# Even spacing of early attention scores among the dense matmuls

## The chip, the cores and the metric

The kernel runs on one core of a Trainium2 chip. A core has a matrix engine (PE, with its weight loads listed as PEld), a vector engine (DVE), a scalar engine (ACT), a general engine (POOL), and a queue that mostly issues DMAs (SP). They run their own instruction streams and wait for each other by semaphores. Matmul results land in PSUM, which is cut into eight banks of 128 x 512 fp32; only DVE and ACT can read them out. The metric is the device time of one execution in microseconds; less is better.

## The reference, cut to what matters

One attention block and one dense block with a gate, over the same normalised input of 2048 tokens by 512:

```python
xn  = layernorm(x)                                  # 2048 x 512
q, k, v = split(xn @ wqkv, heads=32)                # 16 wide each
p   = softmax(q @ k.T * 16 ** -0.5)                 # 32 heads, 2048 x 2048
s   = (p @ v).reshape(2048, 512) @ wo
h   = gelu(xn @ w1 + b1)                            # 2048 x 1376
g   = silu(h @ w2 + b2)
out = x + s * g
```

All of it is fp32. The kernel holds that precision by splitting an operand into a high and a low part and adding three products (high x high, high x low, low x high).

## The kernel before, in words

The softmax needs the maximum of each row of scores before the exponentials. The kernel therefore makes every block of scores twice: once with the queries on the PSUM partitions, only to take row maxima (the *score matmuls*, `s_mm`, line 184, read by a DVE max over 128 x 512, `s_max`, line 190), and once with the keys on the partitions, with the maxima folded in, for the exponentials on ACT (`t_one`, lines 716 and 718).

There are two large stages. In the *dense stage* PE does the value projection, the remaining query and key projections and both dense layers. In the *attention stage* it makes scores, exponentials and the products with the values. The row maxima of the first nine of 32 units (a unit is four heads by 512 queries) are made early, spread through the dense stage: `LEAD = 144` counts the blocks, and each block takes four score matmuls, two heads of a pair and two pairs, so 4 x 144 = 576 *early score tiles*.

A dense matmul contracts over 64 rows, half of the array, and its two halves run as two streams, *row tile* 0 (operand partitions 0 to 63) and row tile 1 (64 to 127). The function `run` (line 595) takes two lists of dense matmuls, one for each row tile, and issues them by turns: one for tile 0, one for tile 1, and so on. Ahead of each it calls `fill(a)` (line 564) with the tile `a` whose turn it is; `fill` may put in one early score on that row tile, which contracts over 48 rows. It does so when the count of what has been issued reaches a due value, and when it is that tile's turn among the scores (`made[0] <= made[1]` picks tile 0, otherwise tile 1), so that even scores are on tile 0 and odd ones on tile 1. `mm` (line 584) issues the dense matmul (line 590) and counts it; where a dense sum was last written by the other row tile and no early score since proves that write done, it first puts in an empty PE instruction that waits for it.

A score tile is written to one of two PSUM banks by turns (`s_ring`, line 91). Each score thus needs the bank that the score two before it used, and its weight load waits on PE until DVE has taken that one's max. The ring is the only link between the scores and DVE.

When the maxima of two units are complete, `s_end0` (line 239) reduces them and queues a transpose that `fill` puts in place of a score some scores later (`later`, `s_end1`, line 268); it takes the next bank of the ring, ACT reads it out (`s_end2`, line 276), and SP stores it to a scratch in DRAM (`mh_d`, line 279), which the attention stage loads (line 152). Four of these fall into the dense stage. `put` raises the due value for each of them.

The due value before is made from `ROWS`, the count of row-half slots in the whole stage, 12 steps for each half of each projection pair, 6 for each part of the second layer, and the scores themselves. Each tile has its own count `row[a]`, which dense matmuls and scores of that tile both raise. The order of everything in the dense stage is thus fixed when the program is built; nothing is decided on the chip.

The other engines in the dense stage: ACT and POOL split weights and hidden activations into high and low parts and read out the sums of the first layer (lines 297, 298, 371, 373, 377, 378), SP loads weights and stores queries and keys. At the end of the stage DVE adds a bias to the last four sums (line 649).

Of the kernel before, what the change touches and what calls it, by code (L numbers as in the profile page):

```python
# [32 lines left out]
LEAD = 144  # L33
NW = 10
EARLY = 4
DONE = 492
FILL0 = 30
HB = 4
W2B = 2
ORDER = {0: "TTTTV", 3: "TSXTTSTYV"}  # L40
# [9 lines left out]
def fused(ctx: ExitStack, tc: tile.TileContext, x, wqk, wv, wo, w1, b1, w2, b2, out):  # L50
# [104 lines left out]
    made = [0, 0]  # L155
# [6 lines left out]
    def tick():  # L162
        for e in later:
            e[0] -= 1
# [39 lines left out]
    def s_one(a):  # L204
        made[a] += 1
        s_whole(heads[made[a] - 1], a)
# [58 lines left out]
    def s_end1(u):  # L265
        pm = s_tile()[0] if "seen" in prog or u == NU - 1 else t_tile()
        n = 2 * GH * NCH * len(units_of(u))
        nc.tensor.matmul(pm[:n, :P], NM.pop(u).rearrange("p u i a -> p (u i a)"), ident_r, start=True, stop=True)
        MH[u] = pm

    def s_end2(u):
        us = units_of(u)
        n = 2 * GH * NCH * len(us)
        mh = qring.tile([4 * GH * NCH, P], F32, name="mh", bufs=1)
        if "seen" in prog:
            nc.scalar.activation(mh[:n], MH.pop(u)[:n, :P], AF.Copy)
        else:
            nc.vector.tensor_copy(mh[:n], MH.pop(u)[:n, :P])
        nc.sync.dma_start(mh_d[us[0]:us[-1] + 1].rearrange("u i j (q s) -> (u i j q) s", s=P), mh[:n])
        sent.update(us)  # L280
# [21 lines left out]
    VQ = 3  # L302
    first = [[("v", t // NCH, t % NCH) for t in range(i, i + 4)] for i in range(NT - 4 * VQ, NT, 4)]
    qs = [(2, 0), (2, 2)] + [(g, 0) for g in range(3, NG)] + [(g, 2) for g in range(3, NG)]
    nu, pairs = len(ms) // 2, []
# [7 lines left out]
    plan, nd = [("first", g, i) for g in range(VQ - 1) for i in (0, 2)], 0  # L313
    for j in range(len(pairs)):
        for h in range(2):
# [4 lines left out]
            due = next((i for i in range(j, len(pairs)) if is_m[i]), len(pairs))  # L320
# [46 lines left out]
    def evac(us, ph):  # L367
# [6 lines left out]
        for u, raw in zip(us, raws):  # L374
            hh = wk.tile([P, CH], F32R, name="hh", bufs=HB)
            hl = wk.tile([P, CH], F32R, name="hl", bufs=HB)
            nc.scalar.activation(hh, raw, AF.Copy)  # L377
# [179 lines left out]

    prog.update(n=0, pe=0, seen=0)
    writer = {}
    s_when, put, row = [], [0], [0, 0]  # L560
    ndown = sum(1 for e in plan if e[0] == "down")
    ROWS = 12 * (4 * VQ + 2 * len(pairs)) + 6 * ndown - 10 + 2 * LEAD - 2 * (LEAD // 32) - FILL0

    def fill(a):
        due = FILL0 + put[0] + sum(made) * ROWS // (4 * LEAD)
        if sum(made) < 4 * LEAD and row[a] >= due and (made[0] <= made[1]) == (a == 0):
            taken()
            if later and later[0][0] <= 0:
                put[0] += 2
                u = later.pop(0)[1]  # L570
                s_end1(u)
                s_end2(u)
                return
            s_one(a)
            row[a] += 1
            tick()

    def taken():
        prog["pe"] += 1
        s_when.append(prog["pe"])  # L580
        if len(s_when) > 2:
            prog["seen"] = max(prog["seen"], s_when[-3])

    def mm(a, key, ps, lhs, rhs, first, last):
        r = slice(64 * a, 64 * a + 64)
        if not first and writer[key][0] != a and writer[key][1] > prog["seen"]:
            hold = nc.tensor.nop().ins
            tc.add_manual_dep(hold, writer[key][2], SYNC, reason="other row tile")
            prog["seen"] = writer[key][1]
        i = nc.tensor.matmul(ps, lhs[r], rhs[r], start=first, stop=last).ins  # L590
        prog["pe"] += 1
        row[a] += 1
        writer[key] = (a, prog["pe"], i.name)

    def run(ops, hooks={}):
        for n, two in enumerate(zip(*ops)):
            prog["n"] += 1
            for a in range(2):
                fill(a)
                mm(a, *two[a])  # L600
            for h in hooks.get(n, []):
                h()
# [448 lines left out]
```

## Time and profile before

| | us |
|---|---|
| median of 3 runs (1572.62 to 1572.99) | 1572.92 |
| the profiled execution | 1573.31 |
| its span, first to last instruction | 1571.4 |
| first to last early score (start) | 58.62 to 471.53 |
| PE, DVE, ACT, POOL busy in the span | 1564.2, 1397.1, 1233.8, 371.9 |
| the 2048 maxes on DVE (line 190) | 1298.8 |

How to read the rows: a timeline row has the start and the length in us, the engine, the line of the kernel, the operation, output and inputs by the program's names, the tile's shapes, and how many instructions were merged (x4). In brackets stands the idle time of that engine just before, and who ended it. Rows of groups have the busy time and the mean in ns of one, then the idle time before them. Ends of matmuls are modelled, so starts are safer to read than ends. Line numbers are those of the kernel before.

### The profile page before, as it was taken

How to read it: one execution, taken by the hardware profiler on the slowest of the kernel's cores; microseconds unless marked ns; L12 is line 12 of the kernel's file. 1: busy time of each engine (PE TensorE's matmuls, PEld its weight loads, DVE VectorE, ACT ScalarE, POOL GpSimd, SP SyncE). 2: the span in 40 equal slices, each digit the busy share in tenths (PEclk: the TensorE clock that was granted, in tenths of full speed). 3: DMA queues.
4: the chain of work that ended last, by engine and by line, in shares of the span. 5: the costliest groups of instructions: out<-in, count | busy, mean ns of one | idle time of the engine just before them, and what ended most of it. 6: DMA issues, size and time to landing. Idle time of an engine off the chain costs nothing.

```text
span 1571.4 us, 31849 instructions
## 1 busy us (share of the span) xinstructions
PE 1564.2 (100%) x12264; PEld 952.0 (61%) x12264; DVE 1397.1 (89%) x2290; ACT 1233.8 (79%) x2397; POOL 371.9 (24%) x394
## 2 busy tenths in 40 slices
PE   9999999999999999999999999999999999999998
PEld 7899999999994444444444444444444444444455
DVE  7599898989988999999999999999999999999834
ACT  4333333333339999999999999999999999999984
POOL 4145575766741001001100100100010000000143
PEclk9999999999999999999999999999999999999999
DMA  6626343454322114111511511321061111110163
GB/s 208 152 59 150 122 139 99 141 152 120 131 84 75 42 30 71 32 36 38 82 32 32 69 33 40 51 52 29 21 81 29 33 29 31 42 30 22 45 199 111
DMA packets 74648, 116.87 MB, mean 74 GB/s; under 512 B 23013, under 2 KB 24293, under 8 KB 73321
## 3 DMA queue, kind: packets, MB, share of 16 engines
q1 hardware_dynamic: 70748, 101.89, 24.1%
q0 software_dynamic: 3264, 12.35, 4.7%
q8 instruction: 97, 1.59, 0.4%
q10 hardware_dynamic: 484, 0.60, 0.1%
q14 instruction: 55, 0.44, 0.1%
HBM read 84.35 MB, written 25.97 MB: 70 GB/s over the span
## 4 chain that ended last, share of the span: by engine, by line
PE 98%; DVE 1%; ACT 0%; DMA 0%; issue 0%; DVEq 0%
PE pv L781 33%; PE pst L716 20%; PE ps L590 13%; PE ps L184 12%; PE pst L590 7%; PE ps L716 6%; PE pv L590 2%; PE ps L905 1%; PE ps L81 1%; PE ps L459 1%; PE pst L81 1%; DVE st L418 0%; PE pst L441 0%; DMA xt<-in_x 0%; PE pst L459 0%
## 5 line engine op out<-in xcount | busy, mean ns | idle before, releaser
L190 DVE TENSOR_REDUCE mx<-ps 128x2 f32<-128x512 f32 x2048 | 1298.8, 685 | 113.7 <-PE ps L184 45.5
L718 ACT ACTIVATE slot<-pst 128x512 f32<-128x512 f32 x1533 | 826.0, 603 | 14.0 <-PE pst L716 7.5
L781 PE MATMUL pv<-slot,vsb 128*32 128x512 f32 x4096 | 545.3, 605 | 0.3 <-DVE os L788 0.3
L716 PE MATMUL pst<-qt,kt 50*128 50x512 f32 x1149 | 380.3, 430 | 0.6 <-DVE gt L649 0.4
L184 PE MATMUL ps<-kt,slot 48*128 48x512 f32 (+1 forms) x1364 | 377.4, 367 | 0.0
L716 PEld LDWEIGHTS pst<-qt,kt 50*128 50x128 f32 x1149 | 191.6, 184 | 256.8 <-ACT slot L718 240.4
L718 ACT ACTIVATE slot<-ps 128x512 f32<-128x512 f32 x515 | 310.9, 604 | 1.9 <-PE ps L184 0.5
L184 PEld LDWEIGHTS ps<-kt,slot 48*128 48x128 f32 x1364 | 225.5, 184 | 40.3 <-DVE mx L190 35.2
L590 PE MATMUL ps<-slot,w1h 64*128 64x512 f32 x1088 | 217.8, 393 | 0.0
L184 PE MATMUL ps<-kt,qz 48*128 48x512 f32 x512 | 213.7, 417 | 0.0
L184 PE MATMUL ps<-slot,slot 48*128 48x512 f32 (+1 forms) x598 | 165.7, 366 | 0.0
L716 PE MATMUL ps<-qt,kt 50*128 50x512 f32 x387 | 160.0, 416 | 0.0
L590 PEld LDWEIGHTS ps<-slot,w1h 64*128 64x128 f32 x1088 | 154.4, 185 | 4.6
L590 PE MATMUL ps<-slot,w1l 64*128 64x512 f32 x544 | 142.0, 393 | 0.0
L781 PEld LDWEIGHTS pv<-slot,vsb 128*32 128x32 f32 x4096 | 80.7, 108 | 100.3 <-issue 92.3
L378 POOL TENSOR_TENSOR hl<-hg,hh 128x512 fp32r<-128x512 f32 x76 | 96.8, 1296 | 151.5 <-ACT hh L377 99.7
L371 ACT ACTIVATE hg<-ps,b_sb 128x512 f32<-128x512 f32 x44 | 27.8, 684 | 132.7 <-PE ps L590 116.9
L251 POOL CAST nmh<-nm 128x16 fp32r<-128x16 f32 x32 | 6.3, 196 | 489.1 <-DVE nm L248 466.6
L716 PE MATMUL pst<-qt,slot 50*128 50x512 f32 x384 | 111.3, 415 | 0.0
L184 PEld LDWEIGHTS ps<-slot,slot 48*128 48x128 f32 x598 | 98.8, 184 | 17.2 <-DVE mx L190 15.2
L184 PEld LDWEIGHTS ps<-kt,qz 48*128 48x128 f32 x512 | 93.7, 183 | 18.7
L716 PEld LDWEIGHTS ps<-qt,kt 50*128 50x128 f32 x387 | 71.1, 184 | 37.5 <-ACT slot L718 31.9
(165 smaller groups left out, 1715.7 us busy)
## 6 DMA issues: line engine op xcount, KB each, us to landing
raw<-in_w SPq DMA_DIRECT2D x88, 256.0 KB
qk_h<-hh SPq DMA_DIRECT2D x32, 256.0 KB
qk_l<-hl SPq DMA_DIRECT2D x32, 256.0 KB
qt<-qk_h SPq DMA_DIRECT2D x128, 64.0 KB
slot<-qk_h SPq DMA_DIRECT2D x92, 64.0 KB
g_d<-gt POOLq DMA_DIRECT2D x16, 256.0 KB, 3.5
qt<-qk_l SPq DMA_DIRECT2D x64, 64.0 KB
dn<-den_d SPq DMA_DIRECT2D x32, 128.0 KB
```

Of the source, the lines that this page charges most:

```text
L81: nc.tensor.matmul(ps, lhs[a], rhs[b], start=first and n == 0, stop=last and n == 2)
L184: return nc.tensor.matmul(ps[:, c0:c0 + w], QS[u][r, p, qi * P:(qi + 1) * P], kts[u // NCH % KB][p][r, k0:k0 + w], start=True, stop=True).ins
L190: nc.vector.tensor_reduce(MX[u][:, 2 * p:2 * p + 2, qi, ki][:, heads, parts], ps.rearrange("p (n c) -> p n c", c=HC), axis=AX.X, op=OP.max)
L251: nc.gpsimd.tensor_copy(hl[:, 0], nm)
L371: nc.scalar.activation(raw, ph.pop(u), AF.Gelu_apprx_tanh, bias=b1_sb[:, u[2]:u[2] + 1])
L378: nc.gpsimd.tensor_sub(hl, raw, hh.bitcast(F32))
L459: nc.tensor.matmul(pq["q", g, c], W1[g][i][:, k * P:(k + 1) * P], (xh, xl)[j][c][:, k], start=n == 0 and k == 0, stop=n == 2 and k == KT - 1)
L590: i = nc.tensor.matmul(ps, lhs[r], rhs[r], start=first, stop=last).ins
L716: nc.tensor.matmul(ps, kts[g % KB][p][r, k * P:(k + 1) * P], QT[u][r, p, :], start=True, stop=True)
L718: nc.scalar.activation(PT[u, k][:, 2 * p + a, :], ps, AF.Exp, scale=SCALE)
L781: nc.tensor.matmul(PV[u][32 * j:32 * j + 32, :], vsb[:, k, h:h + 32], PT[u, k][:, j, :], start=(k == 0), stop=(k == NT - 1))
L905: HALF[0] = nc.tensor.matmul(PW[i][0], OTS[i, k][x][r], (wo_h, wo_l)[y][r, k], start=k == 0 and side == 0 and n == 0, stop=k == KT - 1 and ...
```

## The change

The rule by which `fill` puts a score in is replaced. Before, each row tile has a count of what was issued on it, its scores included, and a score is due at 30 plus 3 for each score made (the value of `ROWS // (4 * LEAD)`) plus 2 for each transpose. After, there is one count, of the dense matmuls of both tiles, and a score or a transpose is due at 60 plus `APART = 5` for each of either made. The alternation between row tiles, the scores' order, the ring and everything else are as they were.

```diff
+APART = 5
...
-    s_when, put, row = [], [0], [0, 0]
-    ndown = sum(1 for e in plan if e[0] == "down")
-    ROWS = 12 * (4 * VQ + 2 * len(pairs)) + 6 * ndown - 10 + 2 * LEAD - 2 * (LEAD // 32) - FILL0
-
+    s_when, put, row = [], [0], [0]
     def fill(a):
-        due = FILL0 + put[0] + sum(made) * ROWS // (4 * LEAD)
-        if sum(made) < 4 * LEAD and row[a] >= due and (made[0] <= made[1]) == (a == 0):
+        due = 2 * FILL0 + APART * (put[0] + sum(made))
+        if sum(made) < 4 * LEAD and row[0] >= due and (made[0] <= made[1]) == (a == 0):
             taken()
             if later and later[0][0] <= 0:
-                put[0] += 2
+                put[0] += 1
                 u = later.pop(0)[1]
                 s_end1(u)
                 s_end2(u)
                 return
             s_one(a)
-            row[a] += 1
             tick()
...
         prog["pe"] += 1
-        row[a] += 1
+        row[0] += 1
         writer[key] = (a, prog["pe"], i.name)
```

## The prediction

> **What bounds the kernel now.** I read the page first, then the busy time by stages, then the groups of one stage, then its timeline engine by engine.
>
> ```profile
> span 1571.4 us, 31849 instructions
> ...
> PE 1564.2 (100%) x12264; PEld 952.0 (61%) x12264; DVE 1397.1 (89%) x2290; ACT 1233.8 (79%) x2397; POOL 371.9 (24%) x394
> ...
> PE 98%; DVE 1%; ACT 0%; DMA 0%; issue 0%; DVEq 0%
> ```
>
> PE is on the chain that ended last for 98% of the span, but a busy PE row only says that some matmul was in flight. The change touches the dense stage alone, so the span is cut there.
>
> ```profile
> 58.60:471.50 412.90, 412.90 (x3473) 378.63 (x3471) 371.50 (x583) 143.52 (x263) 234.55 (x206) 1.00 0.42 120
> ...
> 474.80:1571.40 1096.60, 1091.79 (x8444) 522.91 (x8440) 990.77 (x1621) 1061.17 (x2080) 112.40 (x157) 1.00 0.23 50
> ```
>
> The columns are PE, PEld, DVE, ACT and POOL busy, each with its count, then clock, DMA share and GB/s. The first stretch runs from the first early score to the last: 412.9 us at full clock, ACT and POOL far from full, DVE at 371.5 (90%). The second is the attention phase, which the change leaves as it is.
>
> ```profile
> L190 DVE TENSOR_REDUCE mx<-ps 128x2 f32<-128x512 f32 x576 | 371.7, 686 | 56.6 <-PE ps L184 18.4 <-PE ps L590 7.8 <-PE pst L590 3.5
> ```
>
> In the stage each of the 576 scores has a max on DVE, and DVE idles 56.6 us before them (15.5 of it before the first). So neither engine is full: PE waits for DVE, DVE for PE. How shows in 2 us of the stage.
>
> ```profile
> 300.30 0.42 PE L184 MATMUL ps<-kt,qz 48*128 48x512 f32 x1
> 300.41 0.39 PE L590 MATMUL pst<-w2l,hh 64*128 64x512 f32 x1
> 300.56 0.39 PE L590 MATMUL pv<-w2l,hh 64*128 64x512 f32 x1
> ...
> 300.79 0.39 PE L590 MATMUL pv<-w2h,hl 64*128 64x512 f32 x1
> 300.87 0.44 PE L184 MATMUL ps<-kt,qz 48*128 48x512 f32 x1
> 301.02 0.52 PE L590 MATMUL pst<-w2h,hh 64*128 64x512 f32 x2
> 301.26 0.52 PE L590 MATMUL pst<-w2l,hh 64*128 64x512 f32 x2
> 301.49 0.52 PE L590 MATMUL pst<-w2h,hl 64*128 64x512 f32 x2
> 301.72 0.40 PE L184 MATMUL ps<-kt,qz 48*128 48x512 f32 x1
> ...
> 302.32 0.40 PE L184 MATMUL ps<-kt,qz 48*128 48x512 f32 x1
> ```
>
> Two streams run side by side, one on each half of the array's rows (row tile 0 and 1). The score at 300.30 and the one at 301.72 are on tile 1. Its stream starts at 300.30, 300.56, 300.79, 301.02, 301.26, 301.49, 301.72: a step of 0.26 behind the score, then five of 1.16/5 = 0.232. A whole round of two scores and ten dense matmuls took 1.42 us, against 6 x 0.232 = 1.39 without the long step. The whole stage says the same once the four places are taken off where a small transpose takes the place of a score:
>
> ```profile
> 156.68 0.41 PE L184 MATMUL ps<-kt,qz 48*128 48x512 f32 x1
> ...
> 158.32 0.28 PE L268 MATMUL ps<-ident_r,nmh 128*64 128x128 f32 x1
> ...
> 159.10 0.39 PE L184 MATMUL ps<-kt,qz 48*128 48x512 f32 x1
> ```
>
> Here a round took 2.42 us, 1.0 more. So 575 gaps in 412.9 - 4.0 us, or 408.9/287.5 = 1.422 us a round.
>
> ```profile
> 58.39 0.18 PEld L184 LDWEIGHTS ps<-kt,qz 48*128 48x128 f32 x1
> ...
> 300.21 0.18 PEld L184 LDWEIGHTS ps<-kt,qz 48*128 48x128 f32 x1
> 300.32 0.19 PEld L590 LDWEIGHTS pv<-w2l,hh 64*128 64x128 f32 x1
> ...
> 300.81 0.18 PEld L184 LDWEIGHTS ps<-kt,qz 48*128 48x128 f32 x1
> ...
> 301.62 0.18 PEld L184 LDWEIGHTS ps<-kt,qz 48*128 48x128 f32 x1
> ...
> 302.21 0.18 PEld L184 LDWEIGHTS ps<-kt,qz 48*128 48x128 f32 x1
> ...
> 471.47 0.18 PEld L184 LDWEIGHTS ps<-slot,qz 48*128 48x128 f32 x1
> ```
>
> ```profile
> 299.46 1.29 DVE L190 TENSOR_REDUCE mx<-ps 128x2 f32<-128x512 f32 x2
> ...
> 300.87 1.29 DVE L190 TENSOR_REDUCE mx<-ps 128x2 f32<-128x512 f32 x2
> ...
> 302.31 0.69 DVE L190 TENSOR_REDUCE mx<-ps 128x2 f32<-128x512 f32 x1 [0.15 <-PE ps L590]
> ```
>
> The pair of maxes from 300.87 ends at 300.87 + 1.29 = 302.16, and the next weight load of a score starts at 302.21. The pair before ends at 300.75, the load is at 300.81. The first max of the pair ends at 300.87 + 0.69 = 301.56, the load is at 301.62. Scores own two PSUM buffers, so each load waits for the max two scores back and starts 0.05 us after its end: so do 566 of the 576 loads between the first (58.39) and the last (471.47). A late load is paid by the dense matmul behind it: its own load can start only 0.11 after the score's (300.21, 300.32), and its matmul 0.24 later (300.56). So it starts 0.35 after the score's load, or 0.232 after the score's matmul, whichever is later; a score's load must lead its matmul by 0.12 to cost nothing. The four above lead by 0.09, 0.06, 0.10 and 0.11.
>
> **The change part by part.** The order of the program is counted when it is built; I worked both rules through. Before, ROWS is 1728, so a score is due every 3 counts of its own half, its own scores included: the scores stand ahead of dense matmul 60, 67, 70, 77, 80: gaps of 7 and 3. After, 60, 65, 70, 75: always 5. Even scores (tile 0) stay, odd ones (tile 1) move two dense matmuls ahead. All 576 scores, 2976 dense matmuls and four transposes remain; no instruction, DMA or wait is added or removed; the 12 places where PE waits for the other tile's writer stay 12. On SP and POOL nothing moves but the transpose's read-out and its small store, up to four dense matmuls later (each transpose raises the count by 5 instead of 4).
>
> ```profile
> 435.70 0.45 SPq L279 DMA_DIRECT2D mh_d<-mh  x1
> ...
> 457.70 1.41 SPq L152 DMA_DIRECT2D qt<-mh_d  x2
> ```
>
> I cost that at nothing: the last of these stores is issued 22 us before the first read of what they write, and uncovered it would be 4 x 0.12 = 0.5 us once. The last score has 21 dense matmuls behind it instead of 23:
>
> ```profile
> 471.53 0.43 PE L184 MATMUL ps<-slot,qz 48*128 48x512 f32 x1
> ...
> 474.49 0.69 DVE L649 TENSOR_TENSOR gt<-pv,b_sb 128x512 f32<-128x512 f32 x1 [1.66 <-PE pv L590]
> ```
>
> DVE had been idle 1.66 us ahead of its next work there, which covers the 0.23 by which the last max comes later. So the sum is a matter of the round's length.
>
> Call G the time from a score's matmul to the release of its buffer (start of its max, plus the max, plus 0.05). If every score of a tile is held by its buffer, a round lasts T = (G + 0.35 + 5 x 0.232)/2 = (G + 1.51)/2: the load comes G behind the last score's matmul, and the dense chain runs on from the load. Before, for the score at 300.87: its max is the second of the pair, from 300.87 + 1.29 - 0.69 = 301.47, so 0.60 after the matmul; G = 0.60 + 0.69 + 0.05 = 1.34, T = 1.425. That is the 1.422 measured. Its max is late because DVE is still on the max of the score only three dense matmuls ahead: maxes follow one another no faster than 1.29 - 0.69 = 0.60, the two scores stand 0.57 apart (300.30, 300.87), and the first one's max itself starts 0.57 late.
>
> How soon a max starts that does not queue is seen at the head of the stage, where DVE was idle:
>
> ```profile
> 57.25 0.39 PE L590 MATMUL pv<-kt,slot 64*128 64x512 f32 x1
> ...
> 58.39 0.40 PE L590 MATMUL pv<-kt,slot 64*128 64x512 f32 x1
> ...
> 58.62 0.39 PE L184 MATMUL ps<-kt,qz 48*128 48x512 f32 x1
> ...
> 59.32 0.39 PE L184 MATMUL ps<-kt,qz 48*128 48x512 f32 x1
> ...
> 59.55 0.39 PE L590 MATMUL pst<-kt,slot 64*128 64x512 f32 x1
> 59.55 0.39 PE L590 MATMUL pv<-kt,slot 64*128 64x512 f32 x1
> ```
>
> ```profile
> 59.05 0.69 DVE L190 TENSOR_REDUCE mx<-ps 128x2 f32<-128x512 f32 x1 [15.52 <-PE ps L184]
> ...
> 60.02 0.69 DVE L190 TENSOR_REDUCE mx<-ps 128x2 f32<-128x512 f32 x1 [0.27 <-PE pv L590]
> ```
>
> 58.62 to 59.05: 0.43. But 59.32 to 60.02: 0.70, with DVE idle. The second score is on tile 1, and the dense matmul ahead of it in the program is on tile 0, which ran a step behind and started it only at 59.55. The same holds at 300.30: the dense matmul ahead of it started at 300.41, and the max at 300.87, 0.46 after that. So a score counts as done only when the one ahead of it is, and a lag of tile 0 of 0.11 puts its max 0.57 behind its matmul, with DVE idle (0.15 before 302.31).
>
> The Trainium skill, "TensorE: Matmul & The Clock Gate", Part 3 (packing small matmuls), states that matmuls start and also end in program order. The ends agree with these rows, the starts do not (300.30 stands behind 300.41 in the program). By the whole rule no lag between the tiles could arise, every max would start 0.43 after its matmul, and the new order would give the same 1.39 round as below; where only the ends keep order, the lag is the danger, and it is the slower rival.
>
> With gaps of five, scores stand three steps apart, 0.70, above the 0.60 that DVE needs: no max queues behind another. Then G is 0.43 + 0.69 + 0.05 = 1.17 on the tile that leads, and 1.20 plus the lag on the other. A load leads its matmul by enough when G is at most 1.39 - 0.12 = 1.27, so up to a lag of 0.07. A tile that is not held runs at 1.39; one held by a longer lag runs slower, which shortens its lead over the late tile, so the lag shrinks until neither is held. I take 1.395 (0.2325 a step): 0.027 less a round, times 287.5 = 7.8 us. Bounds: no gain if the lag stays where it is; at most the step of the dense matmuls before any score, (58.39 - 57.25)/5 = 0.228, so 1.368 a round and 15.5 us. I take the step of the stage since it comes from the same mix of matmuls.
>
> Against the profiled execution, 1573.31 us, the sum is 1565.5; that execution lies 0.4 above the median of the runs, so 1565.2 is predicted. The attention phase keeps its 1096.6 us.
>
> **The rivals.**
> - The tiles fall into step: 1.368 a round, 1573 - 15.5 = 1557.4. For it: the head of the stage ran so. Against it: steps of 0.232 in all of the stage, in both tiles.
> - Nothing gained: the odd scores' maxes started late with DVE idle, which more room on DVE does not mend. If the lag of 0.11 stays, G = 0.57 + 0.69 + 0.05 = 1.31, T = 1.41, a gain of 3.4 us at most; with 0.13 it is 1.42, so between 1569.5 and 1573.
> - Slower: the tiles settle a full step apart, as at 59.32. Then every odd max starts 0.70 after its matmul, G = 1.44, T = 1.475, 0.053 a round more, 15.2 us: 1588. It decides from a max that starts 0.59 behind its matmul. For it: it was seen once, and the odd score stays right behind a tile 0 matmul. Against it: the tile that is held slows down, which closes the lag.
>
> **How the numbers follow.** No change can be told from one of 0.2%, 3.1 us. Chances: the forecast 0.57 (its own range 1562 to 1568, steps of 0.231 to 0.234), in step 0.10, nothing gained 0.15, slower 0.18. Faster is the first two, 0.67, and a hair of the third: 0.68; same 0.14; slower 0.18. The range 1557 to 1573.5 leaves out the slower rival alone.
>
> **What would show it.** In the profile after: score matmuls 0.70 apart throughout; score loads that no longer start 0.05 after a max's end but earlier by their place in the stream; the step behind a score 0.23 like the others; no more pairs of maxes in 1.29 us but each with a short idle; the last dense matmul near 467 instead of 474.7. The prediction is wrong if the loads are still released by the maxes, above all if maxes start 0.6 us or more behind their matmuls.

## The result, and the profile after

| | before | after |
|---|---|---|
| median of six runs, us | 1572.97 | 1567.09 |
| lowest and highest | 1572.62 to 1573.60 | 1566.67 to 1567.32 |
| profiled execution, its span | 1573.31, 1571.4 | 1567.11, 1565.3 |
| first to last early score | 58.62 to 471.53 | 59.14 to 466.08 |
| last dense matmul starts | 474.81 | 469.07 |

The ratio is 0.9962, with a 95% interval of 0.9949 to 0.9975: 5.9 us less, where 7.8 were forecast. The busy time by stages of the kernel after, with the columns of before (PE, PEld, DVE, ACT, POOL busy, clock, DMA share, GB/s):

```profile
59.14:466.10 406.96, 406.96 (x3477) 373.55 (x3474) 392.61 (x583) 144.22 (x264) 234.71 (x206) 1.00 0.42 122
...
469.30:1565.30 1096.00, 1091.29 (x8441) 522.57 (x8439) 990.42 (x1621) 1060.72 (x2079) 112.62 (x157) 1.00 0.22 50
```

The stretch of the early scores went from 412.9 to 407.0 us. The attention phase kept its length, 1096.0 against 1096.6. So all of the gain lies where the change is. DVE's busy time in the stretch rose from 371.5 to 392.6 us, although it has the same 576 maxes to take. The group of the maxes says why (in the lines of the changed kernel the max is L191, the score L185, the dense matmul L587):

```profile
L191 DVE TENSOR_REDUCE mx<-ps 128x2 f32<-128x512 f32 x576 | 392.9, 692 | 29.5 <-PE ps L185 19.1 <-PE ps L587 1.3
```

Before, every second max (283 of them) started 0.084 us before the one ahead had ended, and overlapped time counts once: 576 maxes of 686 ns make 395 us, but only 371.7 us of busy time. Now 253 maxes overlap their neighbour, by 0.022 us in the median, and the idle time is 29.5 us instead of 56.6, 15.5 of it before the first. A busier DVE here is the same work spread out. The timeline of PE after:

```profile
298.66 0.40 PE L185 MATMUL ps<-kt,qz 48*128 48x512 f32 x1
...
299.36 0.39 PE L185 MATMUL ps<-kt,qz 48*128 48x512 f32 x1
...
300.08 0.40 PE L185 MATMUL ps<-kt,qz 48*128 48x512 f32 x1
300.30 0.39 PE L587 MATMUL ps<-slot,w1h 64*128 64x512 f32 x1
300.32 0.40 PE L587 MATMUL ps<-slot,w1l 64*128 64x512 f32 x1
300.53 0.42 PE L587 MATMUL ps<-slot,w1h 64*128 64x512 f32 x2
300.77 0.40 PE L185 MATMUL ps<-kt,qz 48*128 48x512 f32 x1
...
301.49 0.40 PE L185 MATMUL ps<-kt,qz 48*128 48x512 f32 x1
```

The scores stand 0.70, 0.72, 0.69 and 0.72 us apart, where they were 0.57 and 0.85 apart. The two tiles run nearly in step (300.30 and 300.32), where one lagged by 0.11. Its score loads and maxes:

```profile
299.87 0.18 PEld L185 LDWEIGHTS ps<-kt,qz 48*128 48x128 f32 x1
300.57 0.18 PEld L185 LDWEIGHTS ps<-kt,qz 48*128 48x128 f32 x1
301.27 0.18 PEld L185 LDWEIGHTS ps<-kt,qz 48*128 48x128 f32 x1
```

```profile
298.43 1.39 DVE L191 TENSOR_REDUCE mx<-ps 128x2 f32<-128x512 f32 x2
...
299.13 1.39 DVE L191 TENSOR_REDUCE mx<-ps 128x2 f32<-128x512 f32 x2
```

Two maxes take 1.39 us instead of 1.29: the second starts 0.70 behind the first instead of 0.60. The maxes end at 299.82 and 300.52, the loads start at 299.87 and 300.57: still 0.05 behind. But the matmuls of these loads start at 300.08 and 300.77, 0.21 and 0.20 after them, more than the 0.12 that by the prediction's estimate a load must lead by. The table is read from the starts in the trace, over all rounds; a round is ten dense matmuls and two scores. Times are medians in us, except those of the second row.

| | before | after |
|---|---|---|
| a round, those with a transpose left out | 1.420 | 1.398 |
| the same in the mean, tile 0 and 1 | 1.422, 1.424 | 1.398, 1.403 |
| step from a score to the dense matmul behind it, tile 0 and 1 | 0.258, 0.256 | 0.234, 0.234 |
| other steps of a tile | 0.233 | 0.233 |
| score matmul to the start of its max, even and odd scores | 0.605, 0.595 | 0.451, 0.480 |
| lead of a score's load over its matmul | 0.084 | 0.190 |
| loads that start within 0.06 of a max's end, of 576 | 566 | 561 |
| loads that lead by less than 0.12, tile 0 and 1, of 288 each | 268, 255 | 18, 50 |
| start of the dense matmul ahead of an odd score in the program, after the score's | 0.132 | 0.016 |

### The profile page after: what moved, and what is told of

Read it like the earlier page. It is cut to its first block, busy times and chain, and to the rows that moved or that the text cites. A ratio compares the mean times of both kernels' runs of the same rounds, so it can differ in the third digit from the quotient of the medians.

```text
span 1565.3 us, 31851 instructions
## 1 busy us (share of the span) xinstructions
PE 1558.7 (100%) x12264; PEld 947.5 (61%) x12264; DVE 1418.3 (91%) x2290; ACT 1233.9 (79%) x2397; POOL 372.1 (24%) x394
## 4 chain that ended last, share of the span: by engine, by line
PE 99%; DVE 1%; ACT 0%; issue 0%; POOL 0%; DVEq 0%; POOLq 0%
PE pv L778 33%; PE pst L713 20%; PE ps L587 13%; PE ps L185 11%; PE pst L587 7%; PE ps L713 6%; PE pv L587 2%; PE ps L902 1%; PE ps L82 1%; PE ps L460 1%; PE pst L82 1%; PE pv L493 1%; PE pst L442 0%; PE pst L460 0%; ACT slot L715 0%
## 5 line engine op out<-in xcount | busy, mean ns | idle before, releaser
L191 DVE TENSOR_REDUCE mx<-ps 128x2 f32<-128x512 f32 x2048 | 1319.9, 687 | 86.3 <-PE ps L185 42.5
L185 PE MATMUL ps<-kt,slot 48*128 48x512 f32 (+1 forms) x1364 | 377.1, 367 | 0.0
L185 PEld LDWEIGHTS ps<-kt,slot 48*128 48x128 f32 x1364 | 225.6, 184 | 40.4 <-DVE mx L191 35.2
L587 PE MATMUL ps<-slot,w1h 64*128 64x512 f32 x1088 | 218.0, 393 | 0.0
L185 PE MATMUL ps<-kt,qz 48*128 48x512 f32 x512 | 201.7, 394 | 0.0
L185 PE MATMUL ps<-slot,slot 48*128 48x512 f32 (+1 forms) x598 | 165.7, 367 | 0.0
L587 PEld LDWEIGHTS ps<-slot,w1h 64*128 64x128 f32 x1088 | 150.8, 185 | 11.6
L587 PE MATMUL ps<-slot,w1l 64*128 64x512 f32 x544 | 148.2, 392 | 0.0
L185 PEld LDWEIGHTS ps<-slot,slot 48*128 48x128 f32 x598 | 98.8, 184 | 17.0 <-DVE mx L191 15.1
L185 PEld LDWEIGHTS ps<-kt,qz 48*128 48x128 f32 x512 | 93.7, 183 | 0.4
```

Source lines behind the costliest of these rows:

```text
L185: return nc.tensor.matmul(ps[:, c0:c0 + w], QS[u][r, p, qi * P:(qi + 1) * P], kts[u // NCH % KB][p][r, k0:k0 + w], start=True, stop=True).ins
L191: nc.vector.tensor_reduce(MX[u][:, 2 * p:2 * p + 2, qi, ki][:, heads, parts], ps.rearrange("p (n c) -> p n c", c=HC), axis=AX.X, op=OP.max)
```

## Experiments

In the first three the rule of the changed kernel is kept, and only the odd scores are shifted: `d` dense matmuls later, with `d` = 2, -2 and 4. The theory is that of the prediction: a score's max queues on DVE behind that of its near neighbour, the buffer comes free late, and the dense matmul behind the next load pays. Times here and below are medians; ratios are to the kernel before, run on the same chip (1573.2 to 1573.4 us).

```diff
-        due = 2 * FILL0 + APART * (put[0] + sum(made))
+        due = 2 * FILL0 + APART * (put[0] + sum(made)) + d * (sum(made) % 2)
```

**Gaps of 7 and 3 under the new rule** (`d` = 2; called e_73 further down).

> The rule of the change (one count, five for each transpose), but the odd scores put back two dense matmuls, to gaps of 7 and 3. Theory (a score's max queues on DVE behind that of the score three dense matmuls ahead, its buffer comes free late, and the dense matmul behind the next load pays): the round is 1.42 us again, 1573 us. Rival (the gain is from the other count of the transposes): 1567 us.

Measured: 1573.33 us, ratio 1.000 (0.9992 to 1.0009). Undoing only the place of the odd scores gives back the whole time of before. The one count in place of two, and the five in place of four for each transpose, are worth nothing that shows.

**The mirror, 3 and 7** (`d` = -2).

> The mirror: odd scores three dense matmuls behind the even ones, seven ahead of the next. Theory: only the tiles change places; the odd score's max now starts 0.60 us after its matmul behind that of the even one, the round is 1.42 us, 1573 us. Rival (the two dense matmuls by which the odd scores came earlier are what counts, since an earlier score has its max earlier): 1567 us or less.

Measured: 1575.24 us, ratio 1.0013 (1.0004 to 1.0022). Now the odd scores' maxes queue, 0.604 us after their matmuls, and the even ones' start 0.591 after theirs with DVE idle. That the scores come earlier is worth nothing; the distance to the neighbour counts. The 2 us over the theory are not explained: a round is 1.425 us in the mean on tile 0 and 1.431 on tile 1, against 1.422 and 1.424 with 7 and 3, and the rounds with a transpose are longer too (2.66 to 2.89 us on tile 0, against 2.43 to 2.64).

**Gaps of 9 and 1** (`d` = 4).

> Gaps of 9 and 1: the pair of scores one step of the stream apart. Theory: the second max starts 0.46 + 0.60 - 0.23 = 0.83 us after its matmul, G = 0.83 + 0.69 + 0.05 = 1.57, the round (1.57 + 1.51)/2 = 1.54 us, 0.118 more than before, times 287.5 = 34 us: 1607 us. Rival (uneven gaps cost a fixed price): about 1573 us. Rival (the gap's own length, 0.6 against 0.2 us, is lost each round): 1573 + 0.4 * 287.5 = 1690 us.

Measured: 1606.05 us, ratio 1.0209 (1.0193 to 1.0224). The mean round is 1.537 us on both tiles, against 1.54 forecast, so the price is neither fixed nor the difference of the gaps. But the rounds are not those of the forecast, and that the number came so near is partly luck. The two scores of a pair never stand one step (0.23 us) apart: in about half of the rounds they stand 0.46 apart and the even max starts 0.84 behind its matmul, in the other half 0.60 apart and 0.66 behind. The odd max starts 0.68 behind its matmul in the median, not 0.46. And the dense steps that are not behind a score are 0.25 us long in the mean, where they were 0.234, which the theory does not have. What holds is the chain from the max to the load to the matmul, as rows of a pair 0.60 apart show. PE's weight loads:

```profile
300.93 0.18 PEld L185 LDWEIGHTS ps<-kt,qz 48*128 48x128 f32 x1 [0.30 <-DVE mx L191]
```

and the score on PE:

```profile
300.93 0.49 PE L185 MATMUL ps<-kt,qz 48*128 48x512 f32 x1
300.93 0.73 PE L587 MATMUL ps<-slot,w1l 64*128 64x512 f32 x2
```

The load is so late that the weight path idles 0.30 us for the max, and the score's matmul starts with its load, with no lead at all. So it is, within 0.02 us, for 279 of the 576 scores.

**7 and 3, but the odd score ahead of tile 0's dense matmul in the program.** In `run` both `fill` calls come before both dense matmuls, and `d` is 1, so that on each tile the order is that of gaps of 7 and 3:

```diff
             for a in range(2):
                 fill(a)
+            for a in range(2):
                 mm(a, *two[a])
```

> Gaps of 7 and 3 on the streams of the two tiles, as before, but each odd score issued ahead of tile 0's dense matmul of its turn instead of behind it; on each tile the order is that of before. Theory (a score counts as done only when the matmul ahead of it in the program is done, and on tile 0 that one runs late): the odd max starts 0.43 us after its matmul instead of 0.60, the even one behind it 0.43 + 0.60 - 0.47 = 0.56 less the lag, the round falls to 1.40 us, 1566 to 1568 us. Rival (only the spacing of the scores on the tiles counts): 1573 us.

Measured: 1567.04 us, ratio 0.9961 (0.9948 to 0.9973). The scores are as unevenly spaced as before, and the gain is the same as that of the even spacing. PE, then DVE:

```profile
299.68 0.40 PE L185 MATMUL ps<-kt,qz 48*128 48x512 f32 x1
...
300.22 0.40 PE L185 MATMUL ps<-kt,qz 48*128 48x512 f32 x1
...
301.09 0.40 PE L185 MATMUL ps<-kt,qz 48*128 48x512 f32 x1
```

```profile
300.11 2.70 DVE L191 TENSOR_REDUCE mx<-ps 128x2 f32<-128x512 f32 x4
```

The scores stand 0.54 and 0.87 apart, and the odd one's max starts 300.11 - 299.68 = 0.43 behind its matmul, 0.595 before. In the kernel before, the even max started 0.605 behind its matmul, which is 0.595 (the odd max behind its own matmul) + 0.608 (from max to max) - 0.598 (from score to score), all medians. So its queue alone added only 0.01; nearly all of its lateness was handed on from the odd max, which had waited for a dense matmul of the other tile that stood ahead of it in the program. With that wait gone the median of the even max is 0.471 and the step behind a score 0.234. The loss needs both: a late odd max, by the order of ends, and an even score so close behind that DVE has no slack to make it up. Taking away either one frees the loads. The empty PE instructions that wait for the other tile are not the cause: there are 9 here, 12 in the kernels before and after, and 15 in e_73, which takes as long as the kernel before; at gaps of five, 6 of them (odd score ahead, below) gain nothing over 12.

**Half maxes, at 7 and 3 and at gaps of five.**

```diff
-SCALE = DH ** -0.5
+SCALE = 0.1 * DH ** -0.5
...
-        nc.vector.tensor_reduce(MX[u][:, 2 * p:2 * p + 2, qi, ki][:, heads, parts], ps.rearrange("p (n c) -> p n c", c=HC), axis=AX.X, op=OP.max)
+        w = HC // 2 if "seen" in prog else HC
+        nc.vector.tensor_reduce(MX[u][:, 2 * p:2 * p + 2, qi, ki][:, heads, parts], ps[:, :2 * w].rearrange("p (n c) -> p n c", c=w), axis=AX.X, op=OP.max)
```

> Gaps of 7 and 3 (as in e_73), but in the dense stage each max reads only the first 256 columns of its block, and the other 256 are left out of the early row maxima; so that the exponentials stay finite, the scale of the softmax is a tenth. The number and size of all matmuls and exponentials stay. Theory: a max takes some 0.35 us instead of 0.69, none queues, buffers are free 0.3 us earlier, no dense matmul waits behind a score: the round is 1.40 us, 1566 to 1568 us, as with gaps of five. Rival (the uneven order itself costs PE, by the order of the tiles' turns, and DVE only shows it): 1573 us.

> The changed kernel (gaps of five) with the same half maxes and the same scale. Theory: at gaps of five the rounds already run at the step of the dense matmuls, so this takes off nothing more than the few longer steps left: 1565.5 to 1567.5 us. Rival (the buffers still hold the scores at gaps of five and the step of 0.233 is DVE's doing): the step falls to the 0.228 of the stage's head, 6 * 0.005 * 287.5 = 9 us less, 1558 us.

Measured: 1565.96 us, ratio 0.9953 (0.9939 to 0.9966), and 1565.07 us, ratio 0.9948 (0.9936 to 0.9961). With maxes of 0.43 us (0.35 was expected) the uneven order costs 0.9 us against the even one; without the long maxes it is not dear. And at gaps of five the shorter max takes off 2 us, somewhat more than expected: a round is 1.394 and 1.396 us in the mean instead of 1.398 and 1.403, and the step of a tile stays at 0.233. The group of the maxes at 7 and 3 with half maxes:

```profile
L192 DVE TENSOR_REDUCE mx<-ps 128x2 f32<-128x256 f32 x576 | 244.6, 425 | 176.5 <-PE ps L588 72.0 <-PE ps L185 47.4 <-PE pst L588 42.2
```

DVE idles 176.5 us there, and PE goes at the same step, so the rest of the round is not set by DVE's maxes.

**Gaps of five, with the odd score ahead.** The edit to `run` as above, with `d` = -1.

> The changed kernel with each odd score issued ahead of tile 0's dense matmul of its turn (counts of 4 and 6; on each tile the order of the changed kernel). Theory: the odd max no longer waits for a late matmul of tile 0, but at gaps of five little of that is left; the round stays at the 1.40 us of six steps: 1566 to 1567.5 us. Rival (part of the round is still lost to the order of ends): 1.39 us, 3 us less, 1564 us.

Measured: 1566.83 us, ratio 0.9959 (0.9947 to 0.9972); against the changed kernel, 0.26 us less, which lies within the spread of either. The two remedies do not add up: once few loads are late there is little left to free (46 lead by less than 0.12 here, 68 in the changed kernel).

**A small piece of work more on DVE behind each early max.** First a fill, then in its place a reduction; both stand in the dense stage only.

```diff
+    extra = keep.tile([P, 8], F32, name="extra")
...
+        if "seen" in prog:
+            nc.vector.memset(extra, 0.0)
```

> Gaps of 7 and 3 (as in e_73), with a tiny fill of 128x8 on DVE behind each early max. A fill alone took 0.06 us; two maxes then follow one another d = 0.06 to 0.13 us later than 0.60. Theory: the queued max and with it G grow by d, the round by d/2: 0.03 to 0.065 us times 287.5 = 9 to 19 us more than 1573, 1582 to 1592 us. Rival (DVE is only 90% busy, 35 fills a 25 us fit into its idle time): 1573 us.

> The changed kernel with the same fills. Theory: maxes start 0.70 us apart, so a d up to 0.10 queues nothing, and the fill stands behind the release of the buffer: 1567 to 1569 us. Rival (DVE, busier here than before, is the bound at gaps of five): the round grows by twice d, 0.12 to 0.26 us, times 287.5 = 35 us or more: over 1600 us.

Measured: 1574.86 us, ratio 1.001 (1.000 to 1.0019), and 1566.82 us, ratio 0.9959 (0.9945 to 0.9973). The size expected of the fill was wrong. It ran mostly beside the max ahead of it: the second max starts 0.623 behind the first instead of 0.608, so d is 0.015, for which the theory gives 2 us (1575.5). That is too near the rival to tell them apart. At gaps of five the time is that of the changed kernel, and the rival of over 1600 us is out.

Two runs with a fill of 128 x 64 gave no time: with its tile 7.875 KB a partition are left where the tiles of the queries need 8. A reduction that writes into the small tile takes its place:

```diff
-            nc.vector.memset(extra, 0.0)
+            nc.vector.tensor_reduce(extra[:, :1], ident_r[:, :64].bitcast(F32), axis=AX.X, op=OP.max)
```

> Gaps of 7 and 3 (as in e_73), with a small reduction of 128x64 of a constant on DVE behind each early max, in place of the fill. The fill of 128x8 put 0.015 us between two maxes (0.623 instead of 0.608); 56 columns more are taken as 0.058 us more, d = 0.073 or somewhat above. Theory: the round grows by d/2 = 0.037, times 287.5 = 10.5 us: 1584 us, to 1590 if d is 0.12. Rival (it fits into DVE's idle time): 1573 to 1575 us.

> The changed kernel with the same small reductions. Theory: two maxes can follow one another in 0.608 + 0.073 = 0.68 us, under the 0.70 between scores, so nearly nothing queues: 1567 to 1569 us; with d = 0.12 DVE becomes the bound, 0.73 a score, and it is 1585 us. Rival (DVE is the bound at gaps of five whatever d is): 2 * 0.073 * 287.5 = 42 us more, 1609 us.

Measured: 1591.34 us, ratio 1.0116 (1.0099 to 1.0133), and 1581.85 us, ratio 1.0054 (1.0039 to 1.0069). The timeline of DVE with gaps of five shows the size of d:

```profile
300.68 0.69 DVE L192 TENSOR_REDUCE mx<-ps 128x2 f32<-128x512 f32 x1
301.27 0.22 DVE L194 TENSOR_REDUCE extra<-ident_r 128x1 f32<-128x64 f32 x1
301.40 0.69 DVE L192 TENSOR_REDUCE mx<-ps 128x2 f32<-128x512 f32 x1
```

Two maxes are 0.72 us apart (0.724 in the median), so d is 0.116, where 0.073 had been taken. The forecasts of 1584 and 1567 to 1569 us were too low for it; those for a d of 0.12, 1590 and 1585, came near. With the measured size the sums come out. At 7 and 3 the theory makes that (1.34 + 0.116 + 1.51)/2 = 1.483 us a round; the medians are 1.483 and 1.489. That is 0.061 more than 1.422, times 287.5 = 17.5 us over 1573.3, or 1590.8, and 1591.3 was measured. At gaps of five DVE is the bound now: 2 x 0.724 = 1.448 us a round, 0.05 more, 14.4 us over 1567.1, or 1581.5, against 1581.85. So the even spacing left DVE 0.70 - 0.61 = 0.09 us a score, and with 0.116 asked of it the even order loses its margin.

## Why the prediction was right, by its steps

- *The loads are released by the maxes, and a late load is paid by the dense matmul behind it:* right. The step behind a score went from 0.258 to 0.234 us, and the median of the other steps stayed at 0.233. The half maxes at 7 and 3, which bring the release forward and keep the order, gave the gain and 1 us more.
- *The even max is late because it queues, T = (G + 1.51)/2:* right at 7 and 3, 1.42 us, and with the small reductions, 1.48. At 9 and 1 the mean of 1.54 fits, but not the single rounds. And the queue is late mainly because the odd max ahead of it is.
- *The odd max is late by the lag of tile 0, because ends keep the program's order:* right, and of more weight than the prediction gave it. Alone it is worth the full gain (odd score ahead: 1567.04 us).
- *The lag shrinks by itself until neither tile is held:* right in direction. The dense matmul ahead of an odd score started 0.132 after it in the median before, 0.016 after (nine tenths of them between -0.08 and 0.10). The argument gives no reason why it should fall much below 0.07, where no tile is held any more. The slower rival, tiles a full step apart, did not come. With half maxes at gaps of five the same order has a median of 0.153 and the tiles do drift a full step apart (odd maxes up to 0.73 behind their matmuls), at no cost: every score's load leads its matmul by 0.12 or more. That speaks for the late loads as what pulls the tiles together.
- *1.395 us a round, 7.8 us:* a term a little too large, 5.9 us came. The round is 1.398 in the mean on tile 0 and 1.403 on tile 1: 50 of 288 odd loads still lead by less than 0.12. With half maxes, which leave none late, it is 2 us less, near the 7.8. The forecast left these loads out.
- *The tiles fall into step at 0.228, 1557 us:* did not happen. With DVE idle for 176.5 us the step was 0.233 as well. What makes it 0.233 and not 0.228 was not tried.
- *A transpose costs nothing more:* not quite. On tile 0 the four rounds with one took 2.41 us in the mean before and 2.66 after. Of the 0.25 more, 0.116 is the fifth dense matmul in place of four, which is only moved; the rest is about half a us over the four places. On tile 1, 2.29 and 2.38, nothing is left.
- *Score loads no longer start 0.05 after a max's end:* wrong. 561 of 576 still do, and the prediction had named just that as a sign that it is wrong. It was a bad sign: the release still starts the load, but early enough. The sign to look for was the lead over the matmul, 0.084 before and 0.190 after. The sign it gave most weight, maxes 0.6 us or more behind their matmuls, did not come (0.451 and 0.480).
- *Each max with a short idle before it:* not so. They start 0.70 us apart and last 0.69, so 253 of them still begin shortly before the one ahead ends.
- *The last dense matmul near 467:* 469.1. The scores start 0.5 us later, and the rest is the smaller gain.

## What to carry to other kernels

A wait that ends in nearly every round is not yet a cost: ask how far the released instruction leads the point where it is needed. With two buffers between two engines, work that takes 0.61 us and comes in pairs 0.60 apart hands any lateness of the first on to the second, even where the consumer is idle a tenth of the time; spacing the work evenly, or letting the first of the pair finish earlier, both free the ring, and doing both frees hardly more. Where two row tiles run side by side, the place of an instruction in the program against its neighbour on the other tile can be worth as much as its place on its own tile.

## What the runs showed of the hardware that was not expected

A matmul on one row tile starts ahead of one on the other tile that stands before it in the program, but what waits for it gets its release as if only when that one had ended. In the median the odd max starts 0.595 us after its matmul at a lag of 0.132 (before), 0.480 at 0.016 (after), 0.569 at 0.106 and 0.613 at 0.153 (half maxes at 7 and 3 and at gaps of five): 0.46 plus the lag each time. Where the matmul ahead in the program started a full step earlier (odd score ahead), it is 0.432. Moving an instruction by one place in the program, with the order on each tile unchanged, was worth 6 us. And on DVE a small fill of 0.065 us behind a max of 0.69 put only 0.015 us between two maxes, while a reduction of 64 columns put 0.116 there.
